# A fused attention and MLP kernel: fp32 loads and transposes for the first pair, key blocks of 160, V shifted by DMA, and separate TensorE tasks for bias and residual

## The chip, the cores and the metric

The kernel runs on one NeuronCore of a Trainium2 chip. The metric is the device time of one execution in microseconds (us); lower is better. The profile's span, from the first to the last instruction, is 1.7 to 2.2 us shorter than the time. One slow run of the kernel before (249.22 us) is left out of the ratios. Each ratio is the mean time of one kernel's fast runs over that of the kernel before in the same rounds on the same chip, so it is not quite the ratio of the medians that are quoted beside it.

Names: PE is TensorE, ACT is ScalarE, DVE is VectorE, POOL is GpSimd, SP is SyncE.

## The reference, cut to what matters

```python
# q, k, v: (4 batches, 8 heads, 768 tokens, 64); n_global = 8, n_local = 96
scores = q @ k.T / 8 + bias            # bias = -slope[head] * distance
keep   = (key < 8) | (0 <= query - key < 96)
a      = softmax(where(keep, scores, -1e9))
x      = (a @ v), heads side by side    # (4, 768, 512)
# mixer over tokens, rank 32, then an MLP over channels
u      = x + (x.T @ U @ V).T
out    = u + relu(u @ w_ch1) @ w_ch2    # w_ch1: 512x2048, w_ch2: 2048x512
```

A query block of 128 tokens needs its own 128 keys, the last 95 of the block before, and the 8 global keys at the very beginning. All inputs and the output are fp32; the kernel computes in fp16 with fp32 sums.

## The kernel before

The work comes in 16 *pairs* (4 batches, each with 4 pairs of heads). For each pair: K, Q and V are loaded by DMAs that GpSimd issues, and arrive as fp16 (the DMA view lists V with 192.0 KB for a pair); PE transposes K and Q; ScalarE and VectorE copy the transposes out of PSUM; PE computes scores, ScalarE the exponentials, PE the products with V; VectorE normalises; PE adds the mixer. After four pairs, the MLP of the batch follows. It is most of PE's time (177.2 of 234.9 us busy, in L739 and L787). The MLP of one batch is interleaved with the attention of the next. Batch 0 has nothing to be interleaved with, so its attention, the *head* of the kernel, runs alone. I call the start of the first MLP matmul **M1**: after it PE has MLP work to do between the tasks of attention.

A small planner simulates the engines when the kernel is built and fixes the order of the tasks on each engine, by estimated durations and hand-tuned priorities. At run time each engine works in that order. If the next task's input is late, the engine waits: in the trace after, PE stood 2.09 us before one product and started nothing else.

The loads, all on GpSimd, in pieces of 6 tokens x 64 values (1,536 bytes):

```python
nc.gpsimd.dma_start(dst[g.slot], src[b, h0:h0 + 2].rearrange("h (p n) d -> p h (n d)", n=NB))
...
TK = add(PE, 0.38, base, tr(g1, stgk, gk), [tk, c_id16], ...)     # transposes of K, fp16
TQ = add(PE, 0.38, base + 1, tr(g2, stgq, gq), [tq, c_id16], ...)
```

The "off-diagonal" operands: for each block, the 32 first keys (with the global ones) in front, and behind them the last 96 keys of the block before. For keys that is a copy within the partitions, `kO`, on VectorE. For V it is a copy, `vo`, whose first 32 rows are overwritten. In batch 0 it is done by GpSimd:

```python
def koff():
    nc.vector.tensor_copy(ko[:, :, 32:P], ...kt...[:, :, 32:P])
    nc.vector.tensor_copy(ko[:, :, 0:32], kt[:, 0:32].unsqueeze(1).broadcast_to((P, NB - 1, 32)))
...
if eng == POOL:
    nc.gpsimd.tensor_copy(vof, vv[:, :, 0:NB - 1])
    nc.gpsimd.tensor_copy(vof[0:32], vv[0:32, :, 0:1].broadcast_to((32, 2, NB - 1, D1)))
```

In batch 0 the bias is added on PE, as a 128x128-tile product that stands *inside* each score task, ahead of the scores, which use 64x128 tiles:

```python
def sc(...):
    if biased:
        nc.tensor.matmul(t[:, hi, lo:512], ident16, bb, start=True, stop=False, ...)
    ...
    lhs = ko[r, i - 1] if j % 2 == 0 else kt[r, i * P:(i + 1) * P]
    nc.tensor.matmul(t[:, hi, j * P:(j + 1) * P], lhs, qt[r, i * P:(i + 1) * P], start=not biased, ...)
```

The residual products of the mixer (32x128 tiles) stand likewise inside the tasks of the second MLP matmul. While nothing is ready in the head, PE is given *dummy* matmuls on zeros.

The softmax here doesn't subtract the row's maximum and nothing guards it: scores larger than these inputs give would overflow.

## Time and profile before

| | before |
|---|---|
| time, median (range) of 4 runs | 245.44 us (244.71 to 245.75) |
| span of the profiled run | 243.6 us |
| first scores start | 11.12 us |
| M1, the first MLP matmul, starts | 32.25 us |
| last matmul starts | 239.88 us |

These lines of the page of the kernel before give the span, the engines' busy time, and PE's busy tenths and granted clock in 40 slices of about 6 us each.

```profile
span 243.6 us, 4964 instructions
PE 234.9 (96%) x2096; PEld 130.2 (53%) x2096; DVE 107.2 (44%) x222; ACT 109.2 (45%) x139; POOL 81.9 (34%) x106
PE   6799999998999999999999999999999999999994
PEclk9999999999999999999999999999999999999999
```

PE is busy almost throughout at full clock (0.999 granted), so PE bounds the kernel. But "busy" hides two things: dummy matmuls count as busy, and so do the short gaps that a matmul's modelled end covers (a 384-column matmul is listed with 326 ns, and the next one starts 163 ns after it). I therefore counted from the start-to-start intervals in the timeline: 0.163 us for each 384-column matmul, 0.216 for a 512-column one, 0.056 for 128 columns, 0.029 for the 65-column products with V, zero for a dummy, and about 0.095 us each time the tile shape changes. The last is what PE loses between, say, a 128x128-tile and a 64x128-tile matmul: the interval is 0.312 us in place of 0.216 after a 512-column matmul, 0.258 in place of 0.163 after a 384-column one, and 0.126 in place of 0.029 after a 65-column one. I call such a change a **drain**; that is a name for the longer interval, whose cause the trace does not show. With these:

| part of the span, before | us |
|---|---|
| head, up to M1 (21.3 of work and drains, 10.9 lost) | 32.25 |
| M1 to the start of the last matmul: work without drains | 194.3 |
| ... 102 drains of 0.095 | 9.7 |
| ... lost to waits | 3.7 |
| start of the last matmul to the end of the span | 3.7 |

The waits view of PE, kernel before (waited for: us in total, times, longest):

```profile
PE ps L450 <- DMA stgk<-in_k_dram: 1.5, 2, 0.8
PE ps L825 <- POOL zero L275: 1.3, 1, 1.3
PE ps L606 <- POOL x L687: 1.1, 1, 1.1
PE ps L450 <- DMA stgq<-in_q_dram: 0.9, 2, 0.5
```

L450 are the transposes: in the head PE waits for loads of K and Q. The 1.1 us for the cast `x` on GpSimd come at 60 us, where GpSimd itself had been held in order behind a DMA (3.52 us, to 56.39). This is the windows view (busy time and number of instructions of each engine, granted clock, DMA share, GB/s), three of its stretches. The DMA share is the time that the packets took, as a share of 16 engines; it passes 1 here (1.61 to 1.71), so packets overlap.

```profile
core 0: us, PE busy (x) PEld busy (x) DVE busy (x) ACT busy (x) POOL busy (x), PEclk, DMA share, GB/s
...
15.00:20.00 5.00, 5.00 (x119) 3.84 (x115) 3.13 (x6) 4.82 (x7) 3.73 (x6) 1.00 1.61 148
...
40.00:50.00 10.00, 9.26 (x99) 5.88 (x100) 4.36 (x9) 7.16 (x10) 7.98 (x10) 1.00 1.71 184
50.00:60.00 10.00, 8.95 (x81) 5.48 (x79) 3.33 (x8) 5.57 (x7) 4.37 (x7) 1.00 1.63 167
```

PE is busy all of 15 to 20 us, and idle for 0.7 and 1.05 us in the two stretches after 40 us. The timeline shows the end of the head's waiting for loads, and M1 (start, us, engine, line, operation, count):

```profile
10.23 0.53 PE L450 MATMUL ps<-ident,stgq 128*64 128x128 f16 x12
...
11.12 0.23 PE L554 MATMUL ps<-qT,kT 64*128 64x128 f16 x2
...
32.25 0.65 PE L739 MATMUL ps<-uT,w 128*128 128x384 f16 x3
```

The last line is M1.

### The profile page before, as it was taken

To read this page: it belongs to the slowest core of one execution; us is meant where nothing else is said; L and a number is where in the kernel's file an instruction comes from. 1 tells how busy PE (TensorE), PEld (TensorE's weight loads), DVE (VectorE), ACT (ScalarE), POOL (GpSimd) and SP (SyncE) were. 2 spreads that over 40 slices of the span, in tenths; PEclk is the share of its full clock that TensorE was granted. 3 is DMA by queue.
4 is the path that set the end of the run, shared out by engine and by line. 5 is a ranking of instruction groups with operands and counts; after the bars stand their busy time and mean duration, and the time that the engine had idled before them with its cause. 6 is when DMAs were issued, how large, how long until landed. Compare 5 with 4: busy or idle time off the path is not lost.

```text
span 243.6 us, 4964 instructions
## 1 busy us (share of the span) xinstructions
PE 234.9 (96%) x2096; PEld 130.2 (53%) x2096; DVE 107.2 (44%) x222; ACT 109.2 (45%) x139; POOL 81.9 (34%) x106
## 2 busy tenths in 40 slices
PE   6799999998999999999999999999999999999994
PEld 2566665665455546666444456566544456554443
DVE  7829663532666555363467377644321210001121
ACT  2789948763504055856341154677300026650000
POOL 9879864836568312537072002001000000000000
PEclk9999999999999999999999999999999999999999
DMA  6999999999999998949299522000012120001212
GB/s 99 169 187 91 131 206 173 193 169 171 157 169 205 165 183 143 108 56 111 18 128 167 142 80 75 0 3 0 3 43 86 43 86 3 1 0 46 86 43 86
DMA packets 84278, 24.52 MB, mean 101 GB/s; under 512 B 73760, under 2 KB 81280, under 8 KB 84256
## 3 DMA queue, kind: packets, MB, share of 16 engines
q0 software_dynamic: 63680, 13.64, 63.3%
q1 hardware_dynamic: 20576, 10.57, 20.3%
q8 instruction: 16, 0.26, 0.4%
q14 instruction: 6, 0.05, 0.0%
HBM read 27.46 MB, written 6.29 MB: 139 GB/s over the span
## 4 chain that ended last, share of the span: by engine, by line
PE 74%; DMA 13%; POOL 9%; issue 2%; DVE 0%; POOLq 0%
PE ps L787 35%; PE ps L739 26%; DMA vt<-in_v_dram 8%; DMA stgq<-in_q_dram 5%; PE ps L554 3%; PE ps L781 2%; PE ps L606 2%; PE ps L628 2%; PE ps L611 2%; PE ps L627 1%; POOL w L381 1%; POOL vo L502 1%; PE ps L702 1%; POOL vo L503 1%; POOL stgq L345 1%
## 5 line engine op out<-in xcount | busy, mean ns | idle before, releaser
L739 PE MATMUL ps<-uT,w 128*128 128x384 f16 x512 | 88.9, 326 | 0.0
L787 PE MATMUL ps<-w,htr 128*128 128x512 f16 (+1 forms) x400 | 88.3, 371 | 0.0
L756 ACT ACTIVATE htr<-ps 128x768 f16<-128x768 f32 x64 | 51.8, 811 | 50.6 <-PE ps L739 50.5
L739 PEld LDWEIGHTS <-w 128*128 128x128 f16 x512 | 47.7, 98 | 31.8 <-issue 1.0
L566 ACT ACTIVATE ep<-ps 128x1024 f16<-128x1024 f32 (+1 forms) x48 | 45.0, 952 | 36.4 <-PE ps L554 32.4
L787 PEld LDWEIGHTS <-htr 128*128 128x128 f16 x400 | 36.7, 98 | 41.3 <-issue 3.4
L805 DVE TENSOR_TENSOR osb<-ps,x_sb 128x512 f32<-128x512 f32 (+1 forms) x25 | 16.7, 669 | 66.5 <-PE ps L787 66.5
L687 POOL CAST x<-x_sb 128x768 f16<-128x768 f32 x12 | 11.2, 932 | 60.7 <-DVE x_sb L666 60.7
L579 DVE TENSOR_TENSOR ep<-ep,mask 128x1024 f16<-128x1024 f16 x24 | 16.9, 713 | 13.2 <-ACT ep L566 13.0
L351 POOL DMA_DIRECT2D stgk<-in_k_dram x20 | 16.7, 844 | 7.8 <-DMA w<-in_moe_w_ch_dram 3.5
L355 POOL DMA_DIRECT2D vt<-in_v_dram x16 | 16.4, 1028 | 6.4 <-PE ps L628 3.5
L351 POOL DMA_DIRECT2D stgq<-in_q_dram x20 | 16.6, 838 | 4.6 <-DMA vt<-in_v_dram 1.6
L716 DVE CAST uT<-ps 128x384 f16<-128x384 f32 x28 | 14.6, 550 | 7.7 <-PE ps L702 7.7
L666 DVE TENSOR_TENSOR x_sb<-ps,rcp 128x768 f32<-128x768 f32 x16 | 15.3, 956 | 0.5
L554 PE MATMUL ps<-qT,kT 64*128 64x128 f16 x192 | 15.1, 218 | 0.3 <-DVE x_sb L666 0.3
L628 PEld LDWEIGHTS <-ep 128*128 128x128 f16 x192 | 12.5, 97 | 2.1 <-DMA stgk<-in_k_dram 0.2
L628 PE MATMUL ps<-vt,ep 128*128 128x65 f16 x192 | 13.4, 193 | 0.0
L554 PE MATMUL ps<-qT,kO 64*128 64x128 f16 x160 | 13.4, 219 | 0.0
L627 PE MATMUL ps<-vo,ep 128*128 128x65 f16 x160 | 12.0, 193 | 0.0
L695 DVE CAST tmp<-ps 128x128 f16<-128x128 f32 x16 | 4.7, 291 | 15.7 <-PE ps L611 15.6
L554 PEld LDWEIGHTS <-kT 64*128 64x128 f16 x192 | 9.0, 94 | 4.5 <-issue 4.2
L554 PEld LDWEIGHTS <-kO 64*128 64x128 f16 x160 | 7.2, 94 | 7.7 <-issue 7.5
(59 smaller groups left out, 168.1 us busy)
## 6 DMA issues: line engine op xcount, KB each, us to landing
out_dram<-osb SPq DMA_DIRECT2D x23, 256.0 KB, 2.0
w<-in_moe_w_ch_dram POOLq DMA_DIRECT2D x8, 512.0 KB, 9.8
vt<-in_v_dram POOLq DMA_DIRECT2D x16, 192.0 KB, 7.0
stgk<-in_k_dram POOLq DMA_DIRECT2D x20, 96.0 KB, 7.1
stgq<-in_q_dram POOLq DMA_DIRECT2D x20, 96.0 KB, 5.6
stgk<-in_k_dram POOLq DMA_DIRECT2D x6, 192.0 KB, 6.0
stgq<-in_q_dram POOLq DMA_DIRECT2D x6, 192.0 KB, 6.5
out_dram<-osb SPq DMA_DIRECT2D x2, 128.0 KB, 1.7
```

The lines of the kernel that those rows point to most:

```text
L351: nc.gpsimd.dma_start(o[:, :, hi], src[b, h0 + hi].rearrange("(n p) d -> p n d", p=P))
L355: nc.gpsimd.dma_start(vt[gv.slot][:, :, :, 0:D], v[b, h0:h0 + 2].rearrange("h (n p) d -> p h n d", p=P),)
L554: nc.tensor.matmul(t[:, hi, j * P:(j + 1) * P], lhs, qt[r, i * P:(i + 1) * P], start=not biased, stop=True, skip_group_check=biased,)
L566: nc.scalar.activation(ep[gep.slot][:, :, lo:512], ps[:, gsc.slot:gsc.slot + 2, lo:512], AF.Exp, scale=qk_scale)
L579: nc.vector.tensor_tensor(ev, ev, mv, ALU.mult)
L628: nc.tensor.matmul(o, e[:, hi, (j + 1) * P:(j + 2) * P], vv[:, hi, i], start=(i == 0), stop=True)
L666: nc.vector.tensor_tensor(xo, pvo()[:, :, :, 0:D], rcp[p % 2].unsqueeze(3).broadcast_to((P, 2, NB, D)), ALU.mult)
L716: nc.vector.tensor_copy(dst, src)
L739: nc.tensor.matmul(ps[:, g.slot + half, 0:HS], w1[:, dc, jt * P:(jt + 1) * P], ub[:, dc, half * HS:(half + 1) * HS], start=(dc == 0), stop ...
L756: nc.scalar.activation(htr[:, jt].rearrange("p (h c) -> p h c", h=2), ps[:, g.slot:g.slot + 2, 0:HS], AF.Relu)
L787: nc.tensor.matmul(o, htr[:, jc, tt * P:(tt + 1) * P], w2[:, jc, c0:c1], start=False, stop=(jc == NJC - 1),)
L805: nc.vector.tensor_tensor(osb[go.slot][:, c0:c1], ps[:, g.slot, 0:c1 - c0], xb[:, tt, c0:c1], ALU.add)
```

## The change

The intent is to shorten the head and to have fewer drains:

1. K and Q of pair 0 are loaded as fp32 by SyncE, which issues its first load earlier than GpSimd does, and transposed in fp32. Pairs 1 to 3 move up in GpSimd's queue.
2. Keys lie in blocks of 160: the block's 128 keys and, behind them, the 32 first ones. The off-diagonal operand is then a slice, `kt[r, i-1, 32:160]`, and the copy `kO` shrinks to the 32 columns.
3. V's operand has the same new order, 96 rows of the block before and then the 32 first. The 96 rows are now shifted by 32 partitions, by a DMA from SyncE, for all 16 pairs; GpSimd copies only the 32 rows.
4. Bias and residual products are their own PE tasks, so that the planner, which now knows a cost for the change of shape (`switch=0.09`), can put them beside other 128x128-tile work.
5. The mask exponentials of ScalarE move behind batch 0, bias scalings move to VectorE, and about 100 priorities are tuned anew.

```diff
-CFG = {'petr': (4, 5), 'bias_dve': (0, 2)}
+CFG = {'petr': (4, 5), 'VO0': 'S', 'f32': 'kq'}
...
+            if p == 0 and nm in fp32_in:
+                def ldf():
+                    nc.sync.dma_start(*by_token(stg32[i], src))
...
+                        nc.tensor.matmul(
+                            ps[64 * hi:64 * hi + 64, g.slot + t, c * P:(c + 1) * P],
+                            stg32[i][:, hi, n * D:(n + 1) * D],
+                            ident, start=(c == 0), stop=(c == 2), skip_group_check=True,
+                        )
...
+            kt = kT[gkT.slot]
+            nc.vector.tensor_copy(kt[:, 0:NB - 1, P:PK], kt[:, 0:1, 0:32].broadcast_to((P, NB - 1, 32)))
...
+        def vo_sp():
+            nc.sync.dma_start(vo[gv.slot][0:PO], vt[gv.slot][32:P, :, 0:NB - 1])
+
+        def vo_g(eng):
+            return lambda: copy(eng, vo[gv.slot][PO:P], vt[gv.slot][0:32, :, 0:1].broadcast_to((32, 2, NB - 1, D1)))
...
-                if biased:
-                    for hi in range(2):
-                        ...
-                        nc.tensor.matmul(t[:, hi, lo:512], ident16, bb, start=True, stop=False, skip_group_check=True)
...
+                SB = add(PE, 0.33 if s == 0 else 0.44, base + 5 + 3 * s, sbias, ..., name=f"SB{p}.{s}")
...
+                if e == PE and t.mode and not mode:
+                    s = max(s, clock[e] + self.switch)
```

Cut here: the new priorities, the mask and bias tables, the wider evacuation copies, the V replicas written by VectorE, and a last output piece of 128 columns in place of 256.

## The prediction

> **What bounds the kernel now.** The page gives PE 234.9 of 243.6 us busy at a granted clock of 0.999, and the waits view shows it waiting only 5.3 us. But that busy time holds dummy matmuls on zeros (63, before the MLP) and drains. I summed PE's real work from start-to-start intervals in the timeline: 0.163 us per 384-column matmul (512 of them, 83.5 us), 0.216 per 512-column one (83 us), 0.056 and 0.029 for small ones, and about 0.095 us each time the tile shape changes (0.312 against 0.216 after a 512-column matmul).[...] The sum is 224.7 us, of 238.6 between first and last matmul. So 13.9 us are lost: 10.9 before the first MLP matmul (it starts at 32.25 with 21.3 us of real work done), about 3 between 32 and 60 us, nearly nothing later. The end costs 3.4 us.
>
> **What the change does.**
> 1. Fewer shape changes: the built order has 122 in place of 150, as bias and residual products are own tasks, grouped. 28 x 0.095 = 2.7 us of PE time (18 of them after the MLP's start).
> 2. Head. K and Q of pair 0 go out from SyncE at about 0.7 us instead of GpSimd at 1.6 (first packets at 1.9 against 3.1), and pairs 1 to 3 move up in GpSimd's queue. Before, PE waits until 9.1 us for K1 and 10.2 for Q1, and the first scores start at 11.1; I expect 8.3. The fp32 transposes cost more[...] but fall where PE runs zeros; dummies fall to 13.
> 3. ScalarE: 6 bias scalings (0.5 us each) go to VectorE, 8 mask exponentials (0.54 each) after batch 0. Its 12 exponentials of batch 0 should end near 25 us instead of 28.2.
> 4. GpSimd loses V copies (1.5 us per pair to 0.75); VectorE loses key copies, V copies and half the evacuation calls. Off the critical path later, useful in the head.
> 5. Added: 16 V shifts by DMA, K loads in 512-byte pieces. DMA is 90 to 99% busy from 6 to 97 us, and the V-replica copies of before took 6.1 us to land; so a V shift may land 4 to 5 us after issue. I expect about 1 us of the head's gain to go there.
> 6. Tail: last piece of 128 columns, not 256: 0.2 us.
>
> **Sum.** First MLP matmul at 29 us (28 to 30.5) with 20.5 us of real work done, then 201.6 us of real work, 3.5 lost in the middle, 3.2 at the end: span 237.3, time 239.2 us, 2.6% faster. Range 236.5 to 242.0. Chances: faster by over 2% 0.75, within 2% 0.23, slower 0.02.
>
> **What would show each step.** Timeline: first scores near 8.3 us, fp32 transposes at 4.3 to 7, last exponential of batch 0 near 25, first MLP matmul near 29. PE intervals: 28 drains fewer, plain intervals unchanged. After 60 us, PE work shorter by about 1.5 us. DMA view: V shifts landing in 2 to 5 us. Waits view: PE's waits for DMA in the first 11 us gone.
>
> **What would make it wrong.** V shifts landing late (6 us or more), or SyncE held up in order by a V load and keeping transposes or stores behind, so that PE waits between 30 and 60 us;[...] an fp32 transpose much dearer; or, on the other side, the middle's 3 us of waits vanishing too (then 236.5).

The sum came to 29 + 201.6 + 3.5 + 3.2 = 237.3 us of span. For the fp32 transposes the trace after has 4.2 us for the two tensors together; an fp16 tensor's twelve matmuls started within 0.31 us (5.50 to 5.81) in the trace before. The DMA line of the page before shows 90% or more in each slice from 6.1 to 91.4 us, and 80% or more in the one up to 97.4. That the GpSimd copies fall to 0.75 us per pair was read from the trace before too (0.79 and 0.72 us for the two copies, one of which goes).

## The result

| | before | after | predicted |
|---|---|---|---|
| time, median (range) of 4 runs | 245.44 (244.71 to 245.75) | 242.68 (242.14 to 243.01) | 239.2 (236.5 to 242.0) |
| ratio | | 0.989 (0.986 to 0.992) | 0.974 |
| first scores start | 11.12 | 9.98 | 8.3 |
| M1 starts | 32.25 | 34.27 | 29 |
| M1 to start of last matmul | 207.63 | 202.63 | 205.1 |
| start of last matmul to end of span | 3.7 | 3.5 | 3.2 |
| span | 243.6 | 240.4 | 237.3 |

The kernel is about 1% faster: within 2%, and outside the predicted range. All of the gain, and more, came after M1, where 5.0 us went away. The head, which was to be 3.2 us shorter, became 2.0 us **longer**.

The same lines of the page of the kernel after:

```profile
span 240.4 us, 4877 instructions
PE 233.1 (97%) x2070; PEld 130.7 (54%) x2070; DVE 95.5 (40%) x178; ACT 107.7 (45%) x139; POOL 86.0 (36%) x112
PE   7969999999999999999999999999999999999994
PEclk9997999999999999999999999999999999999999
```

There is a 6 in PE's third slice (12 to 18 us), and a 7 in the clock's fourth. Neither was there before. The waits view of PE, after:

```profile
PE ps L703 <- DMA vo<-vt: 2.1, 1, 2.1
PE ps L924 <- POOL zero L309: 1.3, 1, 1.3
PE ps L511 <- DMA stg<-in_k_dram: 0.4, 1, 0.4
```

PE's waits for loads have shrunk to 0.4 us, as was meant. One new wait of 2.1 us stands in their place: the product with the shifted V of the first pair (L703) waits for the DMA that shifts it. The timeline, after:

```profile
4.00 4.51 PE L511 MATMUL ps<-ident,stg 128*64 128x128 f32 x48 [0.38 <-DMA stg<-in_k_dram]
...
9.98 0.40 PE L631 MATMUL ps<-qT,kT 64*128 64x128 f16 x8
...
14.57 0.23 PE L704 MATMUL ps<-vt,ep 128*128 128x65 f16 x2
16.90 0.20 PE L703 MATMUL ps<-vo,ep 128*128 128x65 f16 x1 [2.09 <-DMA vo<-vt]
```

The chain of work that ended last (`--critical --window 0:36`) shows where that DMA comes from (start us, us, what):

```profile
3.26 6.76 DMA vt<-in_v_dram
...
10.10 6.75 DMA vo<-vt
...
16.90 0.20 PE ps L703
...
34.27 1.78 PE ps L823 x10
```

The last line is M1.

V of pair 0 was issued at 3.26 us and landed at 10.02. Its shift was issued at 10.10 and took 6.75 us more. In the kernel before, V landed later, at 11.59 us, but GpSimd then copied it in 1.5 us (11.72 to 13.29), and the product started at 15.95 us: about 1 us *earlier* than after. The tile view of `vo`, after, has the landing times of all 16 shifts:

```profile
L581 SPq DMA_DIRECT2D vo<-vt x16: 589/619/1398, 10.1 to 156.7; - x16
...
DMA to landing us min/median/max: 2.4/5.7/9.5
```

The windows view of the same stretches as before:

```profile
15.00:20.00 5.00, 3.10 (x53) 2.26 (x54) 2.99 (x7) 2.09 (x4) 1.78 (x2) 0.77 1.83 187
...
40.00:50.00 10.00, 10.00 (x100) 6.29 (x98) 4.23 (x8) 7.53 (x11) 4.30 (x6) 1.00 1.41 174
50.00:60.00 10.00, 10.00 (x83) 5.46 (x82) 1.79 (x3) 7.92 (x10) 4.30 (x5) 1.00 1.39 177
```

From 15 to 20 us, PE is busy 3.10 us in place of 5.00, and ScalarE 2.09 in place of 4.82: while PE waits for a DMA, ScalarE gets no new scores. From 40 to 60 us the two idle gaps of before are gone.

By the same accounting as before, M1 to the last matmul is 193.5 us of work, 84 drains (8.0 us) and 1.1 us of waits. Of the 5.0 us saved there, 18 drains are 1.7, waits 2.6, and 0.7 is work done ahead of M1 or no longer done.

One fact makes the rest simple. In the trace after and in those of 13 of the 15 experiments, M1 to the start of the last matmul takes 202.62 or 202.63 us. (The 14th has 202.84, and the 15th changes drains there on purpose.) What follows the start of the last matmul takes 3.1 to 3.6 us. So with this order of tasks **the start of M1 decides the time**, up to half a us of tail, and the experiments ask what sets M1.

### The profile page after: what moved, and what is told of

Its sections match the earlier page's. It is cut to its first block, busy times and chain, and to the rows that moved or that the text cites. A ratio compares the mean times of both kernels' runs of the same rounds, so it can differ in the third digit from the quotient of the medians.

```text
span 240.4 us, 4877 instructions
## 1 busy us (share of the span) xinstructions
PE 233.1 (97%) x2070; PEld 130.7 (54%) x2070; DVE 95.5 (40%) x178; ACT 107.7 (45%) x139; POOL 86.0 (36%) x112
## 4 chain that ended last, share of the span: by engine, by line
PE 90%; DMA 6%; DVE 1%; POOL 1%; issue 0%; POOLq 0%; SPq 0%
PE ps L863 36%; PE ps L823 35%; PE ps L631 5%; DMA vt<-in_v_dram 3%; DMA vo<-vt 3%; PE ps L704 2%; PE ps L682 2%; PE ps L703 2%; PE ps L687 2%; PE ps L783 2%; PE ps L612 1%; PE ps L876 1%; PE ps L499 1%; DVE uT L296 0%; POOL stgk L385 0%
## 5 line engine op out<-in xcount | busy, mean ns | idle before, releaser
L863 PE MATMUL ps<-w,htr 128*128 128x512 f16 (+2 forms) x400 | 89.3, 371 | 0.0
L823 PE MATMUL ps<-uT,w 128*128 128x384 f16 x512 | 87.3, 326 | 0.1
L863 PEld LDWEIGHTS <-htr 128*128 128x128 f16 x400 | 35.9, 98 | 40.6 <-issue 4.1
L895 DVE TENSOR_TENSOR osb<-ps,x_sb 128x512 f32<-128x512 f32 (+2 forms) x25 | 16.7, 669 | 58.7 <-PE ps L863 58.6
L631 PEld LDWEIGHTS <-kT 64*128 64x128 f16 x352 | 10.0, 94 | 12.8 <-issue 11.8
L631 PE MATMUL ps<-qT,kT 64*128 64x128 f16 x352 | 16.6, 220 | 0.0
L296 DVE CAST uT<-ps 128x768 f16<-128x768 f32 (+1 forms) x16 | 13.5, 853 | 6.3 <-PE ps L783 6.3
L298 POOL COPY vo<-vt 32x650 f16<-32x650 f16 x16 | 12.3, 770 | 9.8 <-DMA vt<-in_v_dram 9.5
L294 ACT ACTIVATE uT<-ps 128x384 f16<-128x384 f32 x4 | 2.0, 491 | 28.3 <-PE ps L783 28.3
L703 PE MATMUL ps<-vo,ep 128*128 128x65 f16 x160 | 12.1, 193 | 2.1 <-DMA vo<-vt 2.1
L704 PEld LDWEIGHTS <-ep 128*128 128x128 f16 x192 | 12.7, 97 | 2.4
L703 PEld LDWEIGHTS <-ep 128*128 128x128 f16 x160 | 10.4, 97 | 2.3 <-DMA vo<-vt 2.2
## 6 DMA issues: line engine op xcount, KB each, us to landing
vo<-vt SPq DMA_DIRECT2D x16, 121.9 KB, 5.7
```

The costliest lines, as they stand in the source:

```text
L703: nc.tensor.matmul(o, e[:, hi, j * P:(j + 1) * P], vof[:, hi, i - 1], start=True, stop=False)
L704: nc.tensor.matmul(o, e[:, hi, (j + 1) * P:(j + 2) * P], vv[:, hi, i], start=(i == 0), stop=True)
L823: nc.tensor.matmul(ps[:, g.slot + half, 0:HS], w1[:, dc, jt * P:(jt + 1) * P], ub[:, dc, half * HS:(half + 1) * HS], start=(dc == 0), stop ...
L863: nc.tensor.matmul(o, htr[:, jc, tt * P:(tt + 1) * P], w2[:, jc, c0:c1], start=False, stop=(jc == NJC - 1),)
L895: nc.vector.tensor_tensor(osb[go.slot][:, c0:c1], ps[:, g.slot, 0:c1 - c0], xb[:, tt, c0:c1], ALU.add)
```

## The experiments

All gave the right result. "First score" and "M1" are read from the one profiled run. Changed code is against the kernel after unless said otherwise.

| run | what | median us | ratio (95%) | first score | M1 |
|---|---|---|---|---|---|
| (after) | | 242.68 | 0.989 (0.986 to 0.992) | 9.98 | 34.27 |
| c_after_again | kernel after once more | 243.38 | 0.9925 (0.9886 to 0.9963) | 10.37 | 34.61 |
| e1 | V shift of pair 0 on VectorE | 240.94 | 0.9799 (0.9775 to 0.9824) | 9.94 | 32.09 |
| e2 | stall filled with dummies | 243.13 | 0.9908 (0.9887 to 0.9929) | 10.94 | 34.87 |
| e3 | one more dummy at the start | 243.65 | 0.9903 (0.9870 to 0.9937) | 11.28 | 35.12 |
| e4 | e1 and e3 | 241.43 | 0.9824 (0.9803 to 0.9845) | 11.33 | 33.49 |
| e5 | shifts 0 to 3 on VectorE | 244.76 | 0.9967 (0.9941 to 0.9993) | 11.02 | 36.76 |
| e6 | all 16 shifts on VectorE | 247.58 | 1.0084 (1.0042 to 1.0125) | 11.34 | 39.90 |
| e7 | e5, mixer loads late | 245.05 | 0.9983 (0.9951 to 1.0016) | 10.04 | 37.80 |
| e8 | pair 0 in fp16 again | 242.49 | 0.9867 (0.9828 to 0.9907) | 12.46 | 34.97 |
| e9 | e1, VectorE relieved | 240.87 | 0.9808 (0.9784 to 0.9831) | 10.45 | 32.14 |
| e10 | e9, scores earlier | 241.08 | 0.9827 (0.9802 to 0.9852) | 9.17 | 33.88 |
| e11 | 19 drains put back | 246.13 | 1.0022 (0.9994 to 1.0050) | 11.17 | 35.64 |
| e12 | e9 with shifts 0 and 1 | 240.79 | 0.9803 (0.9772 to 0.9834) | 12.05 | 33.94 |
| e13 | e8 and e1 | 242.34 | 0.9872 (0.9840 to 0.9905) | 12.19 | 33.86 |
| e14 | e10 with shifts 0 and 1 | 241.26 | 0.9839 (0.9798 to 0.9880) | 8.89 | 35.25 |

Together, on one chip each: e1 to e4; e5 to e8; e9 to e11 with c_after_again; e12 to e14.

Take care when you compare two rows of M1. A profile is one run, and not always a typical one: e1's is near the fastest of its runs (239.94 us, median 240.94), e12's and e14's are among the slowest of theirs (241.79 and 243.14). What differs is when the early loads land: V of pair 0 was issued at 3.26 us in all these traces but e8 and e13, and landed between 10.02 and 12.22 us. M1 counted from that landing is far steadier. It is 24.2 to 24.3 us in the kernel after, c_after_again and e11, 23.7 to 23.8 in e2 and e3, and 21.5 to 22.0 in e1, e4, e9, e10 and e12; in the kernel before it was 20.7. In traces of one kind, M1 thus moves with the landing of the loads one for one.

### e1: the late V shift taken away

```diff
         def vo_sp():
+            if p in (0,):
+                for r in range(0, PO, 32):
+                    nc.vector.tensor_copy(vo[gv.slot][r:r + 32], vt[gv.slot][r + 32:r + 64, :, 0:NB - 1])
+                return
             nc.sync.dma_start(vo[gv.slot][0:PO], vt[gv.slot][32:P, :, 0:NB - 1])
```

> The changed kernel with one edit, all orders kept: the V shift of pair 0 is done by VectorE in three copies of 32 partitions instead of by DMA (which landed 6 us after issue). Theory A (the late shift cost the head: PE stands 2.1 us in order, then runs at half clock for 3.4 us): the 2.1 us stall at 14.8 us vanishes, no half-clock window near 18 to 22 us, first MLP matmul at 30 to 31 us instead of 34.3, time 2.5 to 4 us under the changed kernel's 242.7, so about 239 to 240. Rival B (the head and middle are bound by loads, so a wait taken away comes back as another wait before 60 us): first MLP matmul may be earlier, but PE's waits between 32 and 60 us return (2 to 3 us as in the kernel before) and the time stays within 1 us of 242.7.

Measured: the 2.1 us stall is gone, the first product with shifted V starts at 15.31 us in place of 16.90, M1 at 32.09 in place of 34.27, and the ratio is 0.9799 against 0.989 and 0.9925 in the two measurements of the kernel after. The waits view of PE, e1:

```profile
PE ps L499 <- DMA stgq<-in_q_dram: 0.6, 1, 0.6
PE ps L635 <- DVE kT L569: 0.5, 1, 0.5
PE ps L686 <- POOL x L772: 0.5, 1, 0.5
```

No wait is over 0.6 us apart from the initial one for the zeros. M1 was expected at 30 to 31 us, so this run fell short of its own theory too. The late shift is shown to cost about 2.2 us of the head: in these two traces the loads landed alike (V of pair 0 at 10.02 and 10.11 us). The span fell by 2.55 us; the other 0.4 is in the tail, and nothing here explains it. It is also shown that it was not hiding the middle: the waits of 40 to 60 us did not come back, although everything there came 2 us earlier. But M1 is at 32.1, not at 29: the shift is less than half of the head's miss. The chain of work that ended last, e1, shows what now stands in the head:

```profile
2.58 6.00 DMA stgq<-in_q_dram
...
9.19 0.96 DVE qT L296
10.21 0.32 DVE vo L583
...
11.31 0.88 DVE vo L583
12.23 0.22 DVE kT L569
12.50 0.28 PE ps L635 x4
...
32.09 2.76 PE ps L827 x16
```

It starts with the load of Q of pair 1. The three V copies on VectorE (L583) follow, and a key copy stands behind them; PE's 0.5 us wait for `kT` in the waits view is that one.

### e2 and e3: the half clock

The clock's 7 in the fourth slice is a record of 3.41 us at half clock, from 17.7 to 21.1 us, after the stall. In the head's beginning, too, the full clock came later than before: the record of full clock starts at 7.46 us against 4.19, and the fp32 transposes ran through most of the time until then. (In the kernel before, 512-column dummies started 0.427 us apart ahead of that point and 0.217 behind it.) What brings the half clock or ends it, the traces do not show. A rival theory was that the clock, and not the wait, cost the time. e2 fills the stall with ten dummies, right ahead of the first product with V; e3 adds one 512-column dummy at the start of the kernel.

```diff
+            if t.name == "PV0":
+                idle(10, 512, t.acq[0].slot)
```

> The changed kernel with 10 dummy matmuls of 512 columns (2.2 us at full clock) put into PE's stall before the products with V of pair 0; the stall itself stays. It splits theory A: if the half clock after the stall costs by itself, no half-clock window appears near 18 to 22 us and the first MLP matmul comes 1.3 to 1.8 us earlier (about 32.7), time about 241. If the half clock costs nothing (other engines bound that stretch), the time stays within 0.5 us of 242.7.

```diff
-                    idle(int(gap / 0.43), 512, bank)
+                    idle(int(gap / 0.43) + 1, 512, bank)
```

> The changed kernel with 6 instead of 5 dummy matmuls at the very start, so PE is busy without a gap until the fp32 transposes begin. Theory: PE was still at half clock until 7.5 us[...], so the 24 fp32 transposes took 4.2 us instead of about 2.6. With the gap filled full clock comes at about 4 us: transposes end near 6.9 instead of 8.3, first scores at 8.6 to 9 instead of 10.0. If nothing but that head start counts, time falls by 1 us or more; if the late V shift of pair 0 is what the head waits for next, the time falls by under 0.5 us, as that landing does not move.

The forecast of 4 us is an estimate from two traces: in the kernel before, nine dummies stood without a gap and the clock was full at 4.19 us; in the kernel after, five dummies and a gap stood ahead of the transposes, and it was full at 7.46. The 2.6 us are 24 pairs of instructions at 0.109 us, the pace of the trace after at full clock.

The clock's line of the page of e2:

```profile
PEclk9999999999999999999999999999999999999999
```

The clock is full throughout, and the time is the same as the kernel's after (0.9908). From the first score to M1 e2 takes 23.9 us, and the kernel after 24.3. So the half-clock stretch cost about half a us: counted from the landing of V of pair 0, M1 comes at 24.2 to 24.3 us in the three traces with the stretch, and at 23.7 to 23.8 in e2 and e3, which have the late shift without it. Taking the late shift away as well (e1) brings it to 22.0. In e3 the full clock came at 6.48 us (PE still waited 0.3 us ahead of the transposes, for VectorE) and the fp32 transposes ended 0.3 us earlier, at 7.96. Nothing was gained, because PE then waited 0.8 and 0.4 us for K and Q of pair 1, which it takes in order ahead of the first scores (K of pair 1 landed at 8.96 in that run). So the clock explains about 0.5 of e1's 2.2 us, and the wait the rest. e3 was expected to have the full clock at about 4 us; that did not come about.

### e4: both together

> Both edits, V shift of pair 0 on VectorE and one more dummy at the start. Theory A: gains add, first MLP matmul near 29 us, as the prediction had it, time near 237.5 to 239. Rival B: first MLP matmul earlier but waits between 30 and 60 us come back, time 240 or more.

The edit is the two diffs of e1 and e3. Measured 0.9824 in the same rounds in which e1 alone gave 0.9799. The dummy adds nothing to e1.

### e5 and e6: more of the shifts on VectorE

If one late shift costs 2.2 us, do the others cost something too? e5 puts pairs 0 to 3 on VectorE, e6 all 16.

```diff
-            if p in (0,):              # e1
+            if p in (0, 1, 2, 3):      # e5; in e6 range(16)
```

> The changed kernel, orders kept, with the V shifts of all four pairs of batch 0 (not only pair 0) done by VectorE, 3 copies of about 0.33 us each, instead of DMA. In the run with pair 0 alone the shift of pair 1 landed 6.2 us after its issue (13.5 to 19.8) and the products with V of pair 1 began at 20.6 against 18.7 in the kernel before. Theory A (late landings are what the head waits for): products of pair 1 begin at 18 to 19, first MLP matmul at 30 to 31 instead of 32.1, time 239 to 240.5, ratio to before about 0.974. Rival (VectorE, in order, becomes the wait; or the loads themselves): no gain over 0.980.

> The same for all 16 pairs, so no V shift by DMA is left. If the shifts' DMA load hurts the loads of the middle, this is faster than the run with four (by up to 1 us) and the loads of batch 1 land earlier; if shifts off the critical path cost nothing, it equals the run with four within 0.5 us.

Both are slower than e1: 0.9967 and 1.0084, with M1 at 36.76 and 39.90 us. The timeline of VectorE in e5:

```profile
14.77 0.96 DVE L296 COPY qT<-ps 128x768 f16<-128x768 f16 x1 [1.25 <-PE ps L499]
15.76 1.00 DVE L583 COPY vo<-vt 32x650 f16<-32x650 f16 x3
...
23.15 1.57 DVE L583 COPY vo<-vt 32x650 f16<-32x650 f16 x3
```

From 14.77 to 28.8 us VectorE has no gap, and the four shifts, of three copies each (the first at 11.30 us), take 1.0 to 2.0 us each. In the head VectorE has no room for four. After M1 the place of the shifts hardly matters: with all 16 on VectorE that stretch takes 202.84 us in place of 202.63, so e6's further loss lies ahead of M1 too. So in the head a DMA is the better place than VectorE for all but the first shift, which has nothing to hide behind. GpSimd, which copied V in the kernel before, was not tried.

### e7: is it the mixer's loads that delay K and V?

Here the two mixer loads (192 KB) are issued behind the key copy of pair 0, on top of e5.

```diff
+            if t.name == "mixl":
+                continue
+            if t.name == "KO0":
+                nc.vector.memset(uf[:, 0:1, 0:1], 0.0)
+                nc.vector.memset(vf[:, 0:1], 0.0)
+                pl.names["mixl"].fn()
```

> As the run with four shifts on VectorE, and the two mixer loads (U and V factors, 192 KB, which the changed kernel issues right behind Q of pair 0) wait until the keys of pair 0 are done at about 8 us. Theory: K and Q of pair 1 landed only at 7.5 to 9.0 and 8.5 to 10.0 us because the queue of loads ahead of them was no shorter; without the mixer's bytes they land about 1 us earlier, first scores at 9 to 9.5, time 0.5 to 1 us less than the run with four. Rival: landing of pair 1[...] does not move; time the same within 0.5 us.

Measured 0.9983 against e5's 0.9967: no gain. K of pair 1 landed at 7.70 us. That is inside the range that it has over the other runs without this edit (7.46 to 9.70), so nothing can be said about the loads from it.

### e8 and e13: the fp32 first pair undone

e8 loads and transposes pair 0 in fp16 through GpSimd again and leaves everything else of the change.

```diff
-    stg32 = sb("stg32", [P, 2, NB * D], FP32, ...)
+    stg32 = sb("stg32", [P, 2, NB * D], FP16, ...)
-                    nc.sync.dma_start(*by_token(stg32[i], src))
+                    nc.gpsimd.dma_start(*by_token(stg32[i], src))
...                  # transposes: ps16, ident16, is_transpose=True; both loads right behind iota
```

> The changed kernel with its first part undone alone: K and Q of pair 0 loaded with a cast to fp16 through GpSimd and transposed in fp16, all orders else kept (both go first in GpSimd's queue). If the fp32 part gives what it was meant for, this loses 1.5 to 2.5 us: K0 lands at 5.5, Q0 at 7, K1 at 9, first scores at 11 or later, first MLP matmul at about 36, time 244 to 245. If the order of loads is all that sets the head, and the faster landing is eaten by the 4.2 us of fp32 transposes, it loses under 0.7 us.

Measured 0.9867: no slower than the kernel after, although the first scores started 2.5 us later (12.46). Here the shift of V 0 landed at 18.08 us, and M1 was at 34.97. While the late shift is in the way, earlier scores are worth nothing that the intervals (about 1 us either way) would show. e13 is the diff of e8 together with that of e1:

> The fp32 part undone (pair 0 loaded with a cast through GpSimd, transposed in fp16) in the kernel whose V shift of pair 0 is on VectorE. With the late shift in place undoing it changed nothing (0.9867 against 0.989 and 0.9925 for the changed kernel). If the fp32 part's lead was only hidden by the late shift, undoing it now costs 1 to 2 us: ratio 0.984 to 0.988. If it is worth nothing by itself, the ratio stays at 0.980.

Measured 0.9872, against 0.9799 for e1 and, in the same rounds, 0.9803 for e12, which is e1 with three more small edits. So once the late shift is gone, the fp32 first pair is worth about 0.7%, or 1.7 us (0.007 x 245; by the two intervals, an estimate of 0.8 to 2.8). One part of the change bought this, and the other hid it. Part of it may be the clock: PE came to full clock only at 15.27 us in e8 and at 13.04 in e13, and no run separates that from the loads.

### e9, e10, e12 and e14: what else holds M1?

With e1, M1 is at 32.1 us. Four edits looked for the remaining 3 us. All contain e1 and move tasks within the fixed order (`move`; seven more moves of e10 and e14 are cut here); e9 takes two of the four V-replica casts of VectorE out of the head; e10 also puts the first pair's scores ahead of the transposes of pair 1; e12 is e9 with the shift of pair 1 on VectorE as well; e14 is e10 with both shifts there.

```diff
+    for nm in ("vrep2", "vrep3"):
+        move(nm, behind="E03")                                   # e9, e10, e12, e14
+    for nm in ("SB0.1", "SB1.0", "S0.1", "SB0.2", "S0.2"):
+        move(nm, before="TK1")                                   # e10, e14
...
+    move("KO1", before="VO0")                                    # e10, e12, e14
```

> The kernel with the V shift of pair 0 on VectorE, and two of the four V-replica casts (parts 2 and 3, which only the residual products need) moved behind batch 0's evacuations in VectorE's order. Theory (VectorE, in order, is what the head waits for once the late shift is gone; the run with four shifts on VectorE, where it was busy without a gap from 10 to 29 us, lost 3.8 us): taking 1.3 us of casts out of its head brings the first MLP matmul 0.7 to 1.3 us earlier, to about 31, ratio to before about 0.976. Rival (loads set the head): no change from 0.980 within 0.002.

> As the run before, and on PE the bias products and the first two score groups of pair 0 are put ahead of the transposes of pair 1, with their exponentials ahead of pair 1's key evacuation on ScalarE, as pair 1's loads land only at 7.5 to 10 us. If PE's fixed order behind pair 1's loads delays the first scores, they start at 8.6 to 9 us instead of 10 to 11.3, and the first MLP matmul comes up to 1 us earlier still: ratio 0.972 to 0.976. If VectorE or later loads bound the rest of the head, the scores move and the MLP's start does not: same as the run before within 0.002.

> V shifts of pairs 0 and 1 on VectorE, two V-replica casts late, and pair 1's small key copy ahead of the first shift copies, all else as in the changed kernel. If pair 1's shift (landing 6.2 us after issue, at 19.8, with its products at 20.6) is what comes next, products of pair 1 begin near 18.5 and the first MLP matmul at 30.5 to 31.5, ratio 0.974 to 0.978; if not, ratio 0.980 as with pair 0 alone. If VectorE jams, it is above 0.983.

> As the first run of this call, and first scores and exponentials of pair 0 ahead of pair 1's transposes. Alone the early scores started at 9.2 but the first MLP matmul did not come earlier, as products of pair 1 waited for its shift by DMA (1.2 us). With that shift on VectorE the lead may count: ratio down to 0.972; or, if loads of pairs 2 and 3 set the rest, the same as the first run of this call.

None beats e1: 0.9808, 0.9827, 0.9803 and 0.9839. VectorE's casts were not the limit (e9: M1 at 32.14). The most telling is e10. Its first scores start at 9.17 us, the earliest but e14's 8.89, although its loads landed late (K of pair 1 at 9.42 us; in e12, with 9.70, the first scores came at 12.05). Yet M1 comes no earlier: 21.9 us after the landing of V of pair 0, as in e1. (That it is 1.8 us later than e1's on the clock is the loads: V landed at 11.95 us, against 10.11. The medians of the two, 241.08 and 240.94, differ by 0.1.) Two lines of its waits view of PE:

```profile
PE ps L616 <- ACT kT L294: 1.3, 1, 1.3
PE ps L707 <- DMA vo<-vt: 1.2, 1, 1.2
```

PE ran out of work sooner, and waited for the key copy of the next pair and for the V shift of pair 1. The start of the scores by itself does not count; V's arrival and the copies behind it may be what binds soon after, but no run moved V's arrival by itself. e12 had a run in which K of pair 1 landed only at 9.70 us; its first scores came at 12.05, and M1 followed 21.9 us later, against 22.2 in e1. Landing times of the early loads vary that much from run to run, and this limits what a single profile can tell of the head.

### e11: the drains

e11 leaves the head's order alone, and after M1 it puts a matmul task of the MLP between two neighbouring narrow-tile tasks, wherever they stood together. That raises the drains after M1 from 84 to 103.

```diff
+        if a.mode and b.mode and b.name[0] in "SH" and b.name[1] != "B" and c.name[0] == "M":
+            move(b.name, behind=c.name)
```

> The changed kernel with score and mixing products after the MLP's start split up again: where two narrow-tile tasks stand next to each other on PE, one MLP task is put between them, so the shape changes after the first MLP matmul go from 84 back to 103 (102 in the kernel before). Theory: each costs about 0.095 us of pure PE time, so this loses 1.6 to 2.0 us against the changed kernel in the same rounds. Rival (drains overlap with waits): within 0.5 us.

> The changed kernel itself, as a control in the same rounds: ratio 0.987 to 0.991. Its landing of K and Q of pair 1 varies from run to run (7.5 to 9.0 us seen), and with it the first scores (10 to 11.3 us).

M1 to the last matmul is 204.96 us in e11 and 202.63 in the control of the same rounds: 2.3 us for 19 drains. One interval of e11, at 106 us between two matmuls of one shape, is 0.3 us longer than such intervals are, and is no drain; the rest is 2.0 us, or 0.11 each, near the 0.095 of the intervals. (The medians differ by 2.75 us; 1.0 of the difference in the two profiles is in the head.) Drains are thus shown to cost PE time that nothing hides, and grouping the narrow tasks is shown to be a gain. The control also had the stall, of 2.0 us, and its M1 was at 34.61.

## Why the prediction was wrong

It predicted a span of 29 + 201.6 + 3.5 + 3.2 = 237.3 us. Measured in the same terms: 34.27 + 201.5 + 1.1 + 3.5 = 240.4.

**Right.** The drains: 122 in place of 150, 18 of the 28 saved ones after M1, and e11 shows that they are real. PE's work after M1: 201.6 predicted, 201.5 measured, drains included. The plain intervals did not change. PE's waits for loads in the first 11 us went down to 0.4 us in this profile (0.6 in c_after_again, and 2.3 in e11, where the loads landed later). The direction, faster, was right too.

**The step that failed: "a V shift may land 4 to 5 us after issue. I expect about 1 us of the head's gain to go there."** The first shifts took 6.75 and 6.61 us. But the longer landing is only part of the error. The first shift is a link of the first pair's chain: V lands, the shift is issued, and PE stands in order in front of it, with nothing else allowed to run. In the kernel before, the shifted V was ready 1.7 us after V had landed (11.59 to 13.29); with the DMA it took 6.8 us (10.02 to 16.85). With the prediction's own 4 to 5 us this delay would have grown by about 3 us, and it charged 1. Counted on the chain, the shifted V was ready 3.6 us later, although V itself had landed 1.6 us earlier (in this profile; over the other traces it landed at 10.1 to 12.2 us). PE's stall was 2.1 us of it, and e1 shows 2.2 us of M1, the half clock included. The prediction had named this among the things that would make it wrong ("V shifts landing late (6 us or more)"), though with PE waiting between 30 and 60 us; the wait came at 14.8.

In the prediction's terms, M1 was to come 20.7 us after the first scores (8.3 to 29) and came 24.3 us after them; e1 takes 2.1 of these 3.6 us away. The first scores account for the other 1.7 us of M1's 5.3.

**A second term of the head was mis-sized.** First scores came at 9.98 us, not 8.3. The fp32 transposes took 4.2 us together (4.00 to 8.2), where 2.7 were forecast (4.3 to 7), an estimate for which no trace had an fp32 transpose. PE was at half clock until 7.46 us: starts of a pair of instructions were 0.213 us apart until then, and 0.110 or less after. (In the kernel before, nine dummies stood at the start and not five, and the clock was full at 4.2 us; over the traces with the fp32 first pair it came at 5.2 to 8.0.) But the clock was not what held the scores: in e1 it was full at 5.6 us, the transposes ended 0.9 us earlier, and the scores still started at 9.94, because K and Q of pair 1, which PE takes first, came no sooner. And e8 and e10 show that the first scores by themselves were not worth what the prediction gave them: 2.5 us later cost nothing that the intervals show (e8, with the late shift in place), and scores put ahead of pair 1 gained nothing (e10). What goes with M1 is the landing of the loads. What the fp32 pair gives, once V is on time, is about 1.7 us (e13). The last exponential of batch 0 started at 28.76 us, after 27.20 in the kernel before; about 25 was predicted for its end.

**A term on the other side.** 3.5 us were expected to be lost in the middle; 1.1 were. In the kernel before, Q of pair 5 had been issued at 29.4 us behind chunks of MLP weights and landed at 40.4, and GpSimd had been held behind a DMA ahead of a cast at 60 us. In the kernel after, that Q lands at 26.0 us, and GpSimd is not held there. The two traces show this, but no run changed the order of loads alone, so that the new load order is the cause is argued and not shown. e1 shows only that the waits did not vanish because M1 was late. This was luck, as far as the prediction goes: it took 2.4 us off the miss; without it the time would have been about 245 us, as before.

**Still open.** With e1, M1 is at 32.1 us, and 29 was predicted. For these 3 us no single cause was found. In all five traces of e1's kind M1 comes about 22 us after V of pair 0 lands, 1 us more than in the kernel before, and V lands at 10.1 to 12.2 us, hardly earlier than the 11.59 of the kernel before's one profile. So loads that land earlier would be the next thing to try; e7 tried it and did not move them. The chain of e1 goes from Q of pair 1, through VectorE, where the V copies now stand ahead of a key copy, and later through GpSimd's casts, to PE's fixed order: four edits of single links or of a few (e9, e10, e12, e14) gained nothing. That the priorities as a whole were tuned to a different timing is possible; nothing here tests it.

**The best version** is e1: 240.94 us, 2.0% below the kernel before (0.9799, interval 0.9775 to 0.9824, so it is unclear whether it is over 2%), by moving one of 16 shifts. e9 and e12 equal it within their intervals.

## What to carry to other kernels

When a copy is replaced by a DMA, ask for each instance whether something is running in its shadow: here PE waited for one of 16 shifts in the kernel after, the first, and that one cost 2.2 us. Engines that work in a fixed order turn one late operand into a stop of the engine and of those it feeds (2.1 us of PE here, with ScalarE busy 2.09 us in place of 4.82 from 15 to 20 us), so cost a change in the head along the whole chain to the first unlimited work (here M1), not by when the first step starts. The count of tile-shape changes is worth reading on a PE-bound kernel: each was about 0.1 us, and 18 fewer gave 1.7 us.

## What the traces leave open

- What brings the half clock back. A wait of 2.1 us was followed by it in the trace after (14.81 to 16.90 us, half clock from 17.7 to 21.1), and so were waits of 2.0 and 2.3 us in c_after_again and e11. But one of 2.4 us in e3 (16.06 to 18.46) was not. Filling the gap with dummies kept the clock full and left the time within its interval (e2, 0.9908 against 0.989 and 0.9925).
- What sets the landing of a 121.9 KB shift. In the trace after, the shifts after 100 us took 2.4 to 5.2 us, with a DMA share of 0.5 to 1.8 (windows view) while each ran, and those of the first 100 us took 4.4 to 9.5 us, with a share of 1.2 to 2.2. The quickest, 2.4 us, had the lowest share, 0.5. No run varied the share by itself, and the landing time is the number that this change depended on.
- Why the landing of the same early load varies from run to run: K of pair 1 landed between 7.46 and 9.70 us over the runs of variants that leave its issue where it was.
